# The first block's triangular systems in two halves, and eight chunks' key products moved into the loop

## The chip, the cores and the metric

The kernel runs on one core of one Trainium2 chip. The core has five engines with a queue of instructions each, which run side by side and wait for one another by semaphores: TensorE (PE; its weight loads are listed as PEld), VectorE (DVE), ScalarE (ACT), GpSimd (POOL) and SyncE (SP, which here only issues DMAs). Each queue is worked off in order. The metric is the device time of one execution in microseconds, lower is better; the kernel before has a median of 855.91 us over 3 runs (853.34 to 859.94).

## What is computed

Three stages in a row: a delta-rule attention, a mixing stage with a Fourier transform and an MLP, and a second MLP with a spatial gate. The change touches the first alone:

```python
batch, n_heads, seq, head_dim = 4, 8, 768, 48
k_n = k / (norm(k) + 1e-06)
for t in range(S):
    y[:, :, t] = q[t] @ state
    v_old = state @ k_n[t]
    state = state + beta[t] * outer(k_n[t], v[t] - v_old)
```

## The kernel before

The sequence is cut into 12 chunks of 64 tokens for each of 4 batches, 48 chunks in all, numbered in the order of work. Within a chunk the recurrence becomes a triangular system: with the key products A (key times key, scaled and masked), the kernel needs the inverse of a 64 x 64 unit triangular matrix for each head. It gets the two 32 x 32 diagonal blocks on VectorE and puts the 64 x 64 inverse together on TensorE.

Eight chunks make a block, six blocks in all. VectorE inverts the 32 x 32 systems of one block at a time. `prep` gathers them (tile `Cc`) and transposes them so that each partition holds whole systems (tile `Ts`, 32 rows by 32 columns to a partition). `solve` scales them by beta over the squared norm (line 274), then eliminates in 30 steps. Steps with at least 4 rows and columns on a side are a product into `tm` (line 308) and an addition (line 313), each cut into two pieces; the others go column by column (line 286) or row by row (line 292). A last scaling (line 317) and two transposes (line 327) give `Tc`, back with the heads' rows on the partitions. `norms` slips seven small instructions for the key norms between the steps. `root` is the square root that a block needs before its scaling (line 141, ScalarE).

The head of the program runs once. It loads the keys of chunks 0 to 7, multiplies them (line 187), and solves block 0 on VectorE with nothing else in that queue. Beside it TensorE and ScalarE make the query products of chunks 0 to 7 (line 508) and `stage_a` of chunks 8 to 23: key and query products (line 220), and three ScalarE copies for each chunk (lines 195, 196, 226). One 512-column matmul on zeros follows (`busy`, line 492). Then come `mask_q(0)` (line 241) and `prep(1)`.

The loop has iterations t = -3 to 47. In iteration t: `values(t+2)` scales the values by the norms (ScalarE, line 397); `mask_q`; `stage_d(t)` makes the output and the new state (lines 439, 440; copies 448 and 457); `stage_c(t+1)` (line 420) and its VectorE subtraction `cw` (line 421); `stage_a(t+20)` from chunk 24 on (line 222, copies 195 and 196, one VectorE multiplication in line 229); `diag` and `merge` build the 64 x 64 inverses (TensorE 373 and 375 in bank Z; ScalarE 361, 377, 380); `stage_b(t+2)` (line 405, copy 407). The solve of the next block is dealt out over eight iterations by shares, in three places of an iteration (`part`): block 1 over t = -3 to 4. `chain` makes the order of the code the order of each engine's queue, so nothing overtakes anything within an engine.

Two conditions matter below. Block 1's scaling waits for its square root, which stands in ScalarE's queue at the end of iteration -3, behind that iteration's merges. And `solve` starts the gathering of the next block only when the key products of its chunks have been issued:

```python
while seen_a[0] < 8 * blk + 16:
    yield None
yield from prep(blk + 1)
```

For block 1 that is chunk 23. Before the change `seen_a` stands at 24 when the loop starts.

Of the kernel before, what the change touches and what calls it, by code (L numbers as in the profile page):

```python
# [20 lines left out]
C = 64  # L21
# [9 lines left out]
HEAD = 24  # L31
# [35 lines left out]
class Kernel:  # L67
# [36 lines left out]
    def load(self, out, in_):  # L104
        return self.nc.sync.dma_start(out=out, in_=in_)
# [13 lines left out]
    def attention(self, cp, pg, pe, p, x, filler, after_solves):  # L119
# [1 line left out]
        bt = cp.tile([128, NBC * HP], F32, name="bt")  # L121


        mk = cp.tile([128, 4 * C + 34], F32, name="mk")
# [142 lines left out]
        def solve(blk):  # L267
# [62 lines left out]
                    root(blk + 1)  # L330
            Tts[blk] = Tc

        class Spread:


# [12 lines left out]
                    pass  # L348


        qs = [slice(32 * u, 32 * u + 32) for u in range(4)]
        lo, up = qs[::2], qs[1::2]


# [128 lines left out]
        zz = self.bank("pz", [128, 512])  # L483
        nc.vector.memset(zz, 0.0)
        for t in ZS:
            nc.scalar.copy(out=t[:, :, :32], in_=mk[:, 4 * C + 2 :].unsqueeze(1).to_broadcast([128, 8, 32]))
# [593 lines left out]
    def run(self):  # L1080
# [19 lines left out]
        def after_solves():  # L1100
            ce.__exit__(None, None, None)
            e["cdw"], e["dw"] = self.pool("dw", "right")
            self.sc, self.dc = slot(2, [128, 1281]), slot(9, [97, 386])
            e["cu"], e["u"] = self.pool("mlpu", "right")

            def loads():

                self.load(out=self.sc, in_=a["sc"])
                yield
                self.load(out=self.dc, in_=a["dc"])  # L1110
                self.load(out=self.idn, in_=a["idn"])
# [132 lines left out]
def layout(q, k, v, beta, moe_w_ch1, moe_w_ch2, moe2_w_in, moe2_w_spatial, moe2_b_spatial, moe2_w_out):  # L1244
    f = np.float32
    o = {}
# [35 lines left out]
    o["mk"] = np.concatenate([j + i < C, s2, j < i, s2, s >= 32, s < 32, s % 32 == i[:, :32]], 1).astype(f)  # L1282
    o["idn"] = np.eye(128, dtype=f)


# [67 lines left out]
```

## Time and profile before

| | |
|---|---|
| median of 3 runs | 855.91 us (853.34 to 859.94) |
| the profiled execution, its own time | 856.51 us |
| its span, first to last instruction | 854.7 us |
| TensorE busy | 805.6 us (94%) |
| VectorE busy | 617.3 us (72%) |
| ScalarE busy | 417.9 us (49%) |
| GpSimd busy | 5.5 us (1%) |
| mean granted TensorE clock | 0.978 of full speed |

The shares are means over stages with different limits. VectorE is busy almost throughout the first quarter of the span, TensorE almost throughout the second half. The rows below are taken from the first 76 us, with one view of the whole.

### The profile page before, as it was taken

Reading aid. Unit: us, or ns where it says so; the run is one execution under the profiler, and the core shown is the slowest. Engines: PE = TensorE matmul, PEld = TensorE weight load, DVE = VectorE, ACT = ScalarE, POOL = GpSimd, SP = SyncE. Lnnn points to the kernel's source line nnn. Section 1 sums busy time; section 2 is a strip of 40 time slices with the busy share of each in tenths; the row PEclk is TensorE's granted clock in tenths of the full one; section 3 lists DMA queues with packets and bytes.
Section 4 is the critical chain, followed back from the end, with each engine's and each line's share of the span. In section 5 each row is a group of like instructions: output and inputs, shape, how many; then the busy total and the mean of one; then the engine's idle time right before and its main releaser. Section 6 shows DMA issues by size and latency. Waiting matters only on the chain.

```text
span 854.7 us, 24141 instructions
## 1 busy us (share of the span) xinstructions
PE 805.6 (94%) x9965; PEld 768.5 (90%) x9965; DVE 617.3 (72%) x1852; ACT 417.9 (49%) x1062; POOL 5.5 (1%) x38
## 2 busy tenths in 40 slices
PE   7778999888887999999999999999999999999998
PEld 7667888777787999899999999999999899899998
DVE  6999999997968997783654891526688377486563
ACT  2668888876665644232224451223472362543532
POOL 0000000000000000000000000000000000000000
PEclk9869999998999999999999999999999999999999
DMA  9365666556440600001022411121101101102001
GB/s 225 92 173 162 179 173 186 150 154 170 137 144 22 240 2 1 0 1 29 1 72 78 130 31 27 32 62 56 37 1 47 67 9 46 58 18 67 29 0 56
DMA packets 57951, 67.57 MB, mean 79 GB/s; under 512 B 31857, under 2 KB 48978, under 8 KB 57842
## 3 DMA queue, kind: packets, MB, share of 16 engines
q1 hardware_dynamic: 57698, 65.89, 26.8%
q8 instruction: 78, 1.28, 0.6%
q14 instruction: 31, 0.25, 0.1%
q10 hardware_dynamic: 144, 0.15, 0.1%
HBM read 53.62 MB, written 4.72 MB: 68 GB/s over the span
## 4 chain that ended last, share of the span: by engine, by line
PE 67%; DVE 4%; ACT 1%; issue 1%; ACTq 0%
PE bankX L833 17%; PE bankY L846 15%; PE bankX L1031 10%; PE bankX L1011 6%; PE bankX L979 6%; PE bankY L1059 5%; PE bankV L846 2%; PE bankX L646 2%; PE bankZ L1059 1%; PE bankX L662 1%; PE bankY L420 0%; PE bankY L440 0%; PE bankX L818 0%; PE bankY L405 0%; PE bankX L640 0%
## 5 line engine op out<-in xcount | busy, mean ns | idle before, releaser
L846 PE MATMUL bankY<-w,hx 128*128 128x384 f32 x756 | 147.2, 336 | 0.0
L833 PE MATMUL bankX<-uh,w 128*128 128x384 f32 x504 | 137.7, 340 | 0.7 <-DVE ul L755 0.7
L846 PEld LDWEIGHTS bankY<-w,hx 128*128 128x128 f32 x756 | 132.4, 188 | 0.5 <-issue 0.3
L838 DVE SCALAR_TENSOR_TENSOR hx<-bankX,hx 128x384 fp32r<-128x384 f32 x84 | 46.2, 551 | 76.4 <-ACT hx L837 73.7
L837 ACT ACTIVATE hx<-bankX 128x384 fp32r<-128x384 f32 x84 | 41.2, 491 | 115.0 <-PE bankX L833 110.2
L833 PEld LDWEIGHTS bankX<-uh,w 128*128 128x128 f32 x504 | 92.1, 188 | 1.2 <-DVE ul L755 0.9
L1031 PE MATMUL bankX<-w,A 128*128 128x384 f32 x504 | 88.8, 334 | 0.0
L1031 PEld LDWEIGHTS bankX<-w,A 128*128 128x128 f32 x504 | 87.6, 188 | 0.0
L833 PE MATMUL bankX<-ul,w 128*128 128x384 f32 x252 | 85.1, 338 | 0.0
L313 DVE TENSOR_TENSOR Ts<-Ts,tm 128x110 f32<-128x110 f32 (+26 forms) x264 | 59.0, 260 | 0.9
L308 DVE TENSOR_TENSOR tm<-Ts 128x110 f32<-128x110 f32 (+26 forms) x264 | 58.6, 258 | 0.4
L420 PE MATMUL bankY<-gak,WU 64*64 64x112 f32 x704 | 47.2, 276 | 6.3 <-ACT WU L407 3.2
L405 PE MATMUL bankY<-gak,TT 64*64 64x96 f32 x768 | 45.8, 260 | 7.6 <-ACT gak L397 3.1
L440 PE MATMUL bankY<-WU,gak 64*64 64x48 f32 x768 | 51.6, 230 | 1.3 <-ACT x L457 1.1
L1011 PE MATMUL bankX<-xh,s 128*128 128x384 f32 x192 | 50.0, 338 | 0.0
L405 PEld LDWEIGHTS bankY<-gak,TT 64*64 64x64 f32 x768 | 38.0, 143 | 12.2 <-ACT gak L397 3.6
L439 PE MATMUL bankY<-Sb,cw 48*48 48x48 f32 x640 | 38.4, 210 | 11.1 <-DVE cw L421 10.7
L440 PE MATMUL bankY<-Sb,cw 48*64 48x48 f32 x704 | 47.3, 226 | 1.6 <-DVE cw L421 1.4
L1020 ACT CAST u<-hx 128x384 fp32r<-128x384 f32 x32 | 15.8, 514 | 66.1 <-DVE hx L1018 66.1
L833 PEld LDWEIGHTS bankX<-ul,w 128*128 128x128 f32 x252 | 47.3, 188 | 0.0
L439 PE MATMUL bankY<-WU,gak 64*64 64x48 f32 x704 | 45.8, 227 | 0.3 <-issue 0.3
L979 PE MATMUL bankX<-s,xh 128*128 128x512 f32 x144 | 45.9, 395 | 0.0
(219 smaller groups left out, 1806.1 us busy)
## 6 DMA issues: line engine op xcount, KB each, us to landing
kq<-in_kq_dram SPq DMA_DIRECT2D x24, 448.0 KB, 4.2
qt<-in_qt_dram SPq DMA_DIRECT2D x48, 196.0 KB, 4.0
gak<-in_kv_dram SPq DMA_DIRECT2D x48, 192.0 KB, 4.2
w<-in_w_dram SPq DMA_DIRECT2D x24, 384.0 KB, 6.4
out_dram<-x SPq DMA_DIRECT2D x24, 192.0 KB, 1.9
kq<-in_kc_dram SPq DMA_DIRECT2D x8, 448.0 KB, 10.1
x<-x SPq DMA_DIRECT2D x96, 36.0 KB, 1.9
s<-in_wi_dram SPq DMA_DIRECT2D x6, 512.0 KB, 4.1
```

The source lines that it names most:

```text
L308: nc.vector.tensor_tensor(out=tm, in0=T[:, r, k : k + 1].to_broadcast(sh), in1=T[:, k : k + 1, :k].to_broadcast(sh), op=MUL)
L313: nc.vector.tensor_add(o, o, tm)
L405: nc.tensor.matmul(pb[h, hp].rearrange("p t d -> p (t d)"), lhsT=tt[h, o + hp], rhs=kv[h, hp], start=True, stop=True)
L420: nc.tensor.matmul(pc[h, hp], lhsT=w[h, hp, :C], rhs=gas[bc][h, hp, : C + D], start=True, stop=True)
L439: nc.tensor.matmul(ps[C * i : C * i + n - C, hp], lhsT=k[:, C:n], rhs=u, start=not last, stop=end)
L440: nc.tensor.matmul(po[hs[1 - i], hp], lhsT=k[:, :C], rhs=u, start=not last, stop=end)
L833: nc.tensor.matmul(ph, lhsT=w1[f][i][:, c * 128 : c * 128 + 128], rhs=cur[k][:, c], start=(c + j == 0), stop=(c == 2 and j == 2))
L846: nc.tensor.matmul(acc[t], lhsT=hx[i][:, t * 128 : t * 128 + 128], rhs=w2[e][k], start=(e == 0 and j == 0), stop=(e == 11 and j == 2),)
L979: nc.tensor.matmul(pv, lhsT=xT[t][i][:, c, kk * 128 : kk * 128 + 128], rhs=wi[2 * c + 1][k], start=(c + j == 0), stop=(c == 2 and j == 2))
L1011: nc.tensor.matmul(pu, lhsT=wi[2 * c][i][:, f * 128 : f * 128 + 128], rhs=xT[hf][k][:, c], start=(c + j == 0), stop=(c == 2 and j == 2))
L1031: nc.tensor.matmul(acc, lhsT=A[:, m, o, i, kk], rhs=Bo[name, kk][:, k], start=(kk + j == 0), stop=(kk == 2 and j == 2))
L1059: nc.tensor.matmul(po, lhsT=a[:, :128], rhs=wo[f][k], start=(f + j == 0), stop=(f == last and j == 2))
```

## The change

Block 0 alone is solved by a new function `halves`. VectorE inverts the two 16 x 16 diagonal blocks of each 32 x 32 system side by side (14 steps in place of 30, on at most 56 elements a piece); the 16 x 16 square below them is made by TensorE as a product of three matrices. `right` multiplies the key products by the upper inverse and ScalarE scales and masks the result into `Yh`; `left` puts the old columns back through a unit matrix, adds the product of the lower inverse (`V`, a third transpose) with `Yh`, and ScalarE copies the sum into `Tc`. Both work on a quarter of the heads (`q`): quarters 0 and 1 in the head, the others in iterations -3 to -1. `stage_a` of chunks 16 to 23 goes from the head into iterations -3 to 4, one each, ahead of `stage_a(24)` in iteration 4. The loads of chunks 24 to 28 are issued in iterations -3, -2, 0, 2 and 4 instead of -3 to 1. The unit matrix `idn` is loaded early, one column is added to `mk`.

```diff
+        def halves(blk):
+            Tf, T, sq, n0 = preps.pop(blk)
+            dT, r = scale(blk, sq, n0)
...
+            for b in range(2):
+                nc.vector.scalar_tensor_tensor(
+                    out=T2[:, b], in0=T2[:, b], scalar=-1.0, in1=d2[:, b].unsqueeze(1).to_broadcast(sh2), op0=MUL, op1=MUL
+                )
...
+            for k in range(1, 15):
+                ops = []
+                for b in range(2):
+                    t = T2[:, b]
...
+            V = p.tile([128, 32, 32], F32, name="V", bufs=1)
+            nc.gpsimd.memset(V[:, :, :16], 0.0)
+            nc.vector.transpose(out=V[:, :, 16:].rearrange("p g r -> p r g"), in_=T[:, 16:])
...
+            def right(q):
+                py, ys[q] = self.bank("pd", [128, 8, 16]), p.tile([128, 8, 16], F32, name="Yh", bufs=2)
+                for g in range(8):
+                    h = 8 * q + g
+                    for u, us in enumerate(qs):
+                        c = C + 32 * (u % 2)
+                        nc.tensor.matmul(py[us, g], lhsT=gas[blk * 8 + h // 4][us, h % 4, c : c + 32], rhs=Tc[us, h, :16], start=True, stop=True)
+                nc.scalar.activation(ys[q], py, AF.Copy, scale=mk[:, 4 * C + 34 : 4 * C + 35])
+
+            def left(q):
+                pr, y, o = self.bank("pd", [128, 8, 16]), ys.pop(q), Tc[:, 8 * q : 8 * q + 8, :16]
+                for us in qs:
+                    nc.tensor.matmul(pr[us], lhsT=self.idn[us, us], rhs=o[us], start=True, stop=False)
+                for g in range(8):
+                    for us in qs:
+                        nc.tensor.matmul(pr[us, g], lhsT=V[us, 8 * q + g], rhs=y[us, g], start=False, stop=g == 7)
+                nc.scalar.copy(out=o, in_=pr)
...
-        Spread(solve(0), 0).finish()
+        right, left = halves(0)
...
-        for bc in range(8, HEAD):
+        for bc in range(8, 16):
             stage_a(bc)
         busy(CF["last"], 512)
+        for part, q in ((right, 0), (right, 1), (left, 0), (left, 1)):
+            part(q)
...
+        lead = {-3: HEAD, -2: HEAD + 1, 0: HEAD + 2, 2: HEAD + 3, 4: HEAD + 4}
+        rest = {-3: ((right, 2), (right, 3)), -2: ((left, 2),), -1: ((left, 3),)}
...
             part(c2)
+            if t + R <= HEAD:
+                stage_a(t + R - 1)
+                if t in lead:
+                    load_kq(lead[t])
             if HEAD <= t + R < NBC:
                 stage_a(t + R)
-            if t < T0 + CF["kq"]:
-                load_kq(HEAD + t - T0)
+            for half, q in rest.get(t, ()):
+                half(q)
```

The order of instructions moves in three places. The first is VectorE's queue in the head: of before, the start of block 0's elimination (the first of 24 steps with `tm` stands in the last four rows).

```order
L274 SCALAR_TENSOR_TENSOR Ts<-Ts,dT 128x16x16
L274 SCALAR_TENSOR_TENSOR Ts<-Ts,dT 128x512
L286 SCALAR_TENSOR_TENSOR Ts<-Ts 128x30
L286 SCALAR_TENSOR_TENSOR Ts<-Ts 128x29 x2
L286 SCALAR_TENSOR_TENSOR Ts<-Ts 128x28 x3
L162 TENSOR_TENSOR nw<-n_221 128x32
L308 TENSOR_TENSOR tm_242<-Ts 128x52
L308 TENSOR_TENSOR tm_244<-Ts 128x56
L313 TENSOR_TENSOR Ts<-Ts,tm_242 128x13x4
L313 TENSOR_TENSOR Ts<-Ts,tm_244 128x14x4
```

Of the change, the end of the same stretch: the last of its 10 steps with `tm`, the row steps, the scaling, the transposes, and what follows.

```order
L366 TENSOR_TENSOR tm_304<-Ts 128x36
L366 TENSOR_TENSOR tm_306<-Ts 128x36
L372 TENSOR_TENSOR Ts<-Ts,tm_304 128x3x12
L372 TENSOR_TENSOR Ts<-Ts,tm_306 128x3x12
L360 SCALAR_TENSOR_TENSOR Ts<-Ts 128x13 x4
L360 SCALAR_TENSOR_TENSOR Ts<-Ts 128x14 x2
L376 TENSOR_TENSOR Ts<-Ts,dT 128x16x16 x2
L379 STREAM_TRANSPOSE Tc<-Ts 128x16x32 x2
L382 STREAM_TRANSPOSE V<-Ts 128x16x32
L241 TENSOR_TENSOR gak<-gak,mk 128x8x64
```

The queue has 60 rows fewer, all of them here; a third transpose stands ahead of `mask_q(0)`. The second place is ScalarE's queue between the head and block 1's square root (line 141). Of before:

```order
L226 COPY gak<-bankX 128x4x64
L377 ACTIVATE ZS_84<-bankZ 96x8x32
L361 COPY TT_89<-Tc 32x8x32 x2
L377 ACTIVATE ZS_85<-bankZ 96x8x32
L380 COPY TT_89<-bankZ 32x512 x2
L141 ACTIVATE n_747<-sq 128x32
```

Of the change, with the lines of the merges 74 higher (377 is 451, 361 is 435, 380 is 454):

```order
L394 ACTIVATE Yh<-bankY,mk 128x128 x2
L404 COPY Tc<-bankY 128x8x16 x2
L451 ACTIVATE ZS_84<-bankZ 96x8x32
L435 COPY TT_89<-Tc 32x8x32 x2
L195 ACTIVATE gak<-bankX,mk 128x4x32
L196 COPY gak<-bankX 128x4x32
L226 COPY gak<-bankX 128x4x64
L394 ACTIVATE Yh<-bankY,mk 128x128 x2
L451 ACTIVATE ZS_85<-bankZ 96x8x32
L454 COPY TT_89<-bankZ 32x512 x2
L141 ACTIVATE n_799<-sq 128x32
```

Nine more instructions stand between block 0's inverse and the square root. The third place is VectorE's queue in iterations 3 and 4, where block 2 is gathered (line 254). Of before, from the last scaling of block 1 the queue goes on with a gathering, `cw`, a gathering, as the trace's rows below show in time. Of the change, line 495 being `cw`:

```order
L317 TENSOR_TENSOR Ts<-Ts,dT 128x512 [waits DVE_49]
L495 TENSOR_TENSOR cw<-qt,bankY 112x448 [waits DMAHW0_49,PE_49]
L241 TENSOR_TENSOR gak<-gak,mk 128x8x64
L229 TENSOR_TENSOR gak<-bankX,mk 128x4x64 [waits DMAHW1_49,DMAHW5_49,PE_49,Activation_49]
L254 SCALAR_TENSOR_TENSOR Cc<-gak,mk 128x512 x2
L261 STREAM_TRANSPOSE Ts<-Cc 128x1024 [waits DVE_49]
L263 COPY sq<-Ts 128x32 [waits DVE_49]
L327 STREAM_TRANSPOSE Tc<-Ts 128x16x32 x2
```

Both gatherings now stand behind `mask_q(6)` and the multiplication of `stage_a(24)`, because `seen_a` reaches 24 only with `stage_a(23)` in iteration 4.

## Rows read from the trace of the kernel before

**Rows 1.** Windows by stretch: start:end, length, each engine's busy us (instructions), granted clock, DMA.

```profile
15.00:76.00 61.00, 46.77 (x1096) 42.70 (x1098) 58.97 (x265) 40.26 (x131) 1.65 (x12) 0.80 0.54 140
76.00:200.00 124.00, 113.04 (x3366) 100.47 (x3360) 114.25 (x470) 100.60 (x311) 2.63 (x19) 0.97 0.61 169
300.00:855.00 555.00, 548.74 (x3150) 535.50 (x3148) 351.54 (x875) 211.19 (x454) 0.00 (x0) 1.00 0.12 37
```

**Rows 2.** Timeline, VectorE, block 0: start us, us, line, operation, tiles, shapes, count [idle].

```profile
14.72 1.02 DVE L274 SCALAR_TENSOR_TENSOR Ts<-Ts,dT 128x256 f32<-128x256 f32 x2
15.78 1.31 DVE L286 SCALAR_TENSOR_TENSOR Ts<-Ts 128x30 f32<-128x30 f32 x6
17.12 0.34 DVE L308 TENSOR_TENSOR tm<-Ts 128x52 f32<-128x52 f32 x2
17.38 0.33 DVE L313 TENSOR_TENSOR Ts<-Ts,tm 128x52 f32<-128x52 f32 x2
...
36.10 1.97 DVE L327 STREAM_TRANSPOSE Tc<-Ts 128x512 f32<-128x512 f32 x2
37.96 0.65 DVE L241 TENSOR_TENSOR gak<-gak,mk 128x512 f32<-128x512 f32 x1
```

**Rows 3.** Timeline, VectorE, start of block 1, first cw, end of block 1.

```profile
43.52 0.18 DVE L153 TENSOR_SCALAR w<-n 128x32 f32<-128x32 f32 x1 [1.40 <-ACT n L141]
...
57.15 0.61 DVE L421 TENSOR_TENSOR cw<-qt,bankY 112x448 f32<-112x448 f32 x1
...
69.89 0.74 DVE L254 SCALAR_TENSOR_TENSOR Cc<-gak,mk 128x512 f32<-128x512 f32 x1
...
72.78 0.68 DVE L241 TENSOR_TENSOR gak<-gak,mk 128x512 f32<-128x512 f32 x1
73.39 2.10 DVE L327 STREAM_TRANSPOSE Tc<-Ts 128x512 f32<-128x512 f32 x2
...
75.68 0.18 DVE L153 TENSOR_SCALAR w<-n 128x32 f32<-128x32 f32 x1
```

**Rows 4.** Timeline, ScalarE: chunks 15 and 16, then iterations 1 to 4.

```profile
26.03 0.37 ACT L195 ACTIVATE gak<-bankX,mk 128x128 f32<-128x128 f32 x1
...
26.90 0.37 ACT L195 ACTIVATE gak<-bankX,mk 128x128 f32<-128x128 f32 x1
...
59.67 0.32 ACT L448 COPY Sb<-bankY 128x192 f32<-128x192 f32 x1 [3.90 <-PE bankY L440]
...
64.29 1.01 ACT L397 ACTIVATE gak<-gak,n_all 128x48 f32<-128x48 f32 x4
...
67.67 1.01 ACT L397 ACTIVATE gak<-gak,n_all 128x48 f32<-128x48 f32 x4
...
71.60 1.01 ACT L397 ACTIVATE gak<-gak,n_all 128x48 f32<-128x48 f32 x4
...
73.52 0.23 ACT L141 ACTIVATE n<-sq 128x32 f32<-128x32 f32 x1
73.65 0.35 ACT L195 ACTIVATE gak<-bankX,mk 128x128 f32<-128x128 f32 x1
```

**Rows 5.** Windows, merge instructions alone (bank Z); engines PE, PEld, DVE, ACT.

```profile
39.65:41.65 2.00, 1.93 (x64) 1.69 (x64) 0.00 (x0) 0.00 (x0) 0.50 0.62 152
61.50:62.65 1.15, 1.10 (x64) 0.93 (x64) 0.00 (x0) 0.00 (x0) 1.00 0.00 0
```

**Rows 6.** Windows around falls of the granted clock, columns as in Rows 1.

```profile
34.10:37.00 2.90, 0.00 (x0) 0.00 (x0) 2.83 (x9) 0.00 (x0) 0.00 (x0) 1.00 0.00 0
44.00:54.00 10.00, 8.96 (x168) 8.11 (x166) 9.78 (x56) 7.21 (x22) 0.15 (x1) 0.50 0.97 237
54.00:57.70 3.70, 0.00 (x0) 0.00 (x0) 3.70 (x17) 1.73 (x6) 0.00 (x0) 0.96 0.17 44
57.80:60.50 2.70, 2.68 (x72) 2.68 (x74) 2.70 (x15) 0.79 (x3) 0.00 (x0) 0.50 0.65 209
```

**Rows 7.** Timeline, TensorE, the matmul on zeros behind the last head chunk.

```profile
32.90 1.13 PE L492 MATMUL bankY<-TT 128*128 128x512 f32 x2
```

More of the change, by code (lines that the diff above doesn't have):

```diff
@@ L121, in attention @@
         bt = cp.tile([128, NBC * HP], F32, name="bt")
-        mk = cp.tile([128, 4 * C + 34], F32, name="mk")
+        mk = cp.tile([128, 4 * C + 35], F32, name="mk")
         ZS = [cp.tile([128, 8, 64], F32, name=f"ZS{i}") for i in range(2)]
@@ L331, in solve @@
             Tts[blk] = Tc
+        qs = [slice(32 * u, 32 * u + 32) for u in range(4)]
+        def halves(blk):
+            Tf, T, sq, n0 = preps.pop(blk)
+            dT, r = scale(blk, sq, n0)
+            T2 = Tf.rearrange("p (b x) -> p b x", b=2)[:, :, :512].rearrange("p b (i c) -> p b i c", c=32)[:, :, :, :16]
+            d2 = dT.rearrange("p (b i) -> p b i", b=2)
+            sh2 = [128, 16, 16]
+            for b in range(2):
+                nc.vector.scalar_tensor_tensor(
+                    out=T2[:, b], in0=T2[:, b], scalar=-1.0, in1=d2[:, b].unsqueeze(1).to_broadcast(sh2), op0=MUL, op1=MUL
+                )
+            nc.gpsimd.memset(Tf[:, 0:1024:33], 1.0)
+            nc.gpsimd.memset(T[:, 16:, :16], 0.0)
+            newton = norms(blk, sq, n0, r)
+            for k in range(1, 15):
+                ops = []
+                for b in range(2):
+                    t = T2[:, b]
+                    if k < 3:
+                        for c in range(k):
+                            nc.vector.scalar_tensor_tensor(
+                                out=t[:, k + 1 :, c], in0=t[:, k + 1 :, k], scalar=t[:, k, c : c + 1], in1=t[:, k + 1 :, c], op0=MUL, op1=ADD
+                            )
+                    elif k > 12:
+                        for i in range(k + 1, 16):
+                            nc.vector.scalar_tensor_tensor(
+                                out=t[:, i, :k], in0=t[:, k, :k], scalar=t[:, i, k : k + 1], in1=t[:, i, :k], op0=MUL, op1=ADD
+                            )
+                    else:
+                        o, sh = t[:, k + 1 :, :k], [128, 15 - k, k]
+                        tm = pe.tile([128, 256], F32, name=f"tm{b}", bufs=2)[:, : sh[1] * k].rearrange("p (i j) -> p i j", j=k)
+                        nc.vector.tensor_tensor(
+                            out=tm, in0=t[:, k + 1 :, k : k + 1].to_broadcast(sh), in1=t[:, k : k + 1, :k].to_broadcast(sh), op=MUL
+                        )
+                        ops.append((o, tm))
+                next(newton, None)
+                for o, tm in ops:
+                    nc.vector.tensor_add(o, o, tm)
+            for _ in newton:
+                pass
+            for b in range(2):
+                nc.vector.tensor_mul(T2[:, b], T2[:, b], d2[:, b].unsqueeze(2).to_broadcast(sh2))
+            Tc = pg.tile([128, 32, 32], F32, name="Tc", bufs=2)
+            for s in (slice(0, 16), slice(16, 32)):
+                nc.vector.transpose(out=Tc[:, :, s].rearrange("p g j -> p j g"), in_=T.rearrange("p i j -> p j i")[:, s])
+            V = p.tile([128, 32, 32], F32, name="V", bufs=1)
+            nc.gpsimd.memset(V[:, :, :16], 0.0)
+            nc.vector.transpose(out=V[:, :, 16:].rearrange("p g r -> p r g"), in_=T[:, 16:])
+            Tts[blk] = Tc
+            ys = {}
+            def right(q):
[14 more added lines that the diff above has]
+                nc.scalar.copy(out=o, in_=pr)
+            return right, left
@@ L348, in finish @@
                     pass
-        qs = [slice(32 * u, 32 * u + 32) for u in range(4)]
         lo, up = qs[::2], qs[1::2]
@@ L472, in attention @@
             load_kq(8 + 2 * i)
+        load(out=self.idn, in_=a["idn"])
         load(out=qx, in_=a["qx"].rearrange("b p h -> p b h"))
@@ L485, in attention @@
         for t in ZS:
-            nc.scalar.copy(out=t[:, :, :32], in_=mk[:, 4 * C + 2 :].unsqueeze(1).to_broadcast([128, 8, 32]))
+            nc.scalar.copy(out=t[:, :, :32], in_=mk[:, 4 * C + 2 : 4 * C + 34].unsqueeze(1).to_broadcast([128, 8, 32]))
         warm = TT[0].rearrange("p a b -> p (a b)")
@@ L1110, in loads @@
                 self.load(out=self.dc, in_=a["dc"])
-                self.load(out=self.idn, in_=a["idn"])
                 for i in range(CF["ahead"]):
@@ L1281, in layout @@
     j, s2 = KEY[s], np.where(s < 32, (s <= i) & (i < 32), (i < 32) | (s <= i))
-    o["mk"] = np.concatenate([j + i < C, s2, j < i, s2, s >= 32, s < 32, s % 32 == i[:, :32]], 1).astype(f)
+    o["mk"] = np.concatenate([j + i < C, s2, j < i, s2, s >= 32, s < 32, s % 32 == i[:, :32], -(s % 32 >= 16).astype(f)], 1).astype(f)
     o["idn"] = np.eye(128, dtype=f)
```

## The prediction

> **What bounds the kernel now.** I read the windows by stretch first. From 15 to 76 us VectorE is busy 58.97 of 61.00 us, TensorE 46.77 and ScalarE 40.26 [rows 1]; from 76 to 200 us VectorE and TensorE are both near 92%; behind 300 us TensorE alone binds, 548.74 of 555 us. So the change works where VectorE is the bound. The order of every queue is fixed, and behind iteration 4 it is the same as before: what block 2 gains or loses at its start is carried to the end. Transfers don't hold it up there (DMA share 0.12 behind 300 us). The time that counts is therefore the first VectorE instruction of block 2's scaling, at 75.68 us [rows 3], and the question is how much earlier it comes.
>
> Then VectorE's timeline. Block 0's elimination runs from 14.72 to `mask_q(0)` at 37.96 us, 23.24 us without a gap that the reader could fill [rows 2]. The chunks' copies beside it take ScalarE 0.87 us a chunk (26.03 to 26.90) [rows 4], so they hide. Behind it VectorE waits once, 1.40 us, for block 1's square root on ScalarE, and starts block 1 at 43.52 us [rows 3]. That instruction is what the head has to release.
>
> **What VectorE saves in the head.** Two scalings of 512 elements in all, for 768 in 1.06 us: 0.7 us each [rows 2]. Six column instructions, as many as before, 1.24 us; six row instructions the same at most. Forty product and addition instructions of 36 to 56 elements; the rows show two of 52 and 56 elements in 0.26 us, 0.13 each, so 5.2 us, and seven norm instructions among them at most 0.9. Two transposes 1.86 us, the third half of that, 0.93. The sum is 12.8 us at these prices. The operands are smaller than in the rows, which takes off something; if all per-element time were halved it would be about 11.5. I take 12.3, nearer to the rows. `mask_q(0)` then starts at 27.0 instead of 37.96: **11.0 us saved** (10.4 to 11.7). `Tc` is ready at 26.1. The gathering of block 1 behind it needs chunk 15, copied by 26.9, so it doesn't wait.
>
> **What the path to block 1 gains.** TensorE comes off `stage_a(15)` when ScalarE begins to read it, about 26 us. The 512-column matmul of 1.13 us [rows 7], hidden so far behind the elimination, now stands on the path: `right(0)` starts at 27.0, not 26.1. A `right` is 32 matmuls, which the trace lists as 64. Sixty-four merge matmuls on 32 partitions took 1.93 us at 1.2 GHz and 1.10 at 2.4 GHz [rows 5]; they have 32 and 64 columns, these have 16. I take half, 0.55 us, between 0.3 (only columns count) and 1.1 (only the count does). A `left` has four matmuls of 128 columns more: 0.8 (0.5 to 1.4). Two of each are 2.7 us, the last result and its copy 0.6: ready at 30.3.
>
> The Trainium skill ("TensorEngine Tiling (Array Packing)", "Instruction Overhead") has about 60 cycles of overhead on every matmul and says that a shorter free dimension saves nothing below that. By it 16 columns cost as much as 32, the four parts take about 1.1 us more, and the gain worked out below would be 0.5 us. No row of before has 16 columns, so the trace does not decide it.
>
> From `Tc` (36.10 + 1.97 = 38.07) to 43.52 the chain through two merges, `diag` and the square root took 5.45 us, at half clock. At full clock the 64-matmul merge saves 0.83 us [rows 5] and the shorter one about half of it: 4.2. New in that chain on ScalarE are `stage_a(16)`, 0.87, and two `Yh` copies like the first of a chunk's, 0.37 each at most, 0.65 together. So 30.3 + 4.2 + 0.9 + 0.6 gives 36.0: **block 1 starts 7.5 us earlier**, not 11.0. TensorE has no long pause on this way (it was busy from 15 us on), so I take full clock. At half clock the four parts cost 4.8, the merges 5.45, and about 0.7 of `right(2)` and `right(3)` shows: 40.0, only 3.5 us earlier.
>
> **What the loop gives back.** Seven and a half microseconds earlier, `cw(1)` is at 49.65 instead of 57.15 [rows 3]. Until there ScalarE is no limit: it was busy 8.94 of 13.7 us from 44 to 57.7 [rows 6] and gets three chunks (2.6) and two quarter copies (0.6), 12.1 us. TensorE still pauses before `cw(1)`, as at 54.0 to 57.7, where the clock fell afterwards to 1.2 GHz [rows 6]; I take the same fall. ScalarE's copy of the state then starts at 59.67 - 7.5 = 52.2 us.
>
> From there ScalarE decides, and this is the step that costs most. Block 2's gathering was interleaved with iterations 3 and 4; now it stands behind `stage_a(23)` in iteration 4. Before, ScalarE went from 59.67 through 64.29, 67.67 and 71.60 to 73.52, where iteration 4's chunk comes: 4.62 + 3.38 + 3.93 + 1.92 = 13.85 us [rows 4]. Into it go chunks 20, 21 and 22, 3 x 0.87 = 2.6, and the first two copies of chunk 23, about 0.4. So the second gathering can start 16.85 us behind the state copy, at 69.1 us, against 69.89 before. Meanwhile VectorE is done with block 1's steps 7.5 us early and idles for most of that. From the second gathering to the end of block 1's transposes it was 73.39 + 2.10 - 69.89 = 5.6 us, less 0.6 for `mask_q(6)`, which now stands ahead [rows 3]: 5.0. That ends at 74.1. The multiplication of `stage_a(24)` has gone ahead too, so block 2's scaling starts at once, 74.1 instead of 75.68: **1.6 us earlier**.
>
> **Edits at nothing.** GpSimd's new memsets run beside VectorE's steps. The early load of `idn` stands before `qx`, the sign column and the query tiles in SP's queue; its first user is `left(0)` near 28 us, that of the others later. The loads of chunks 24 to 28 wait in SP's queue for TensorE to have read chunks 15, 17, 19, 21 and 23; behind them stand value and query loads. Chunk 24 is wanted near 69 us and its load goes out near 31, so it is covered; if a value load came late instead, `values` would wait and ScalarE's chain would lengthen by as much. The merge behind block 1's transposes still comes after them, so it moves with them.
>
> **The sum.** 856.51 - 1.6 = 854.9 us against the profiled execution; this one is 0.6 above the median of the three runs, so 854.3 on their scale. The runs lie 6.6 us apart, more than the effect.
>
> **Rivals.** *The wait on ScalarE is mostly slack (0.22).* Part of the 13.85 us were waits for TensorE, 3.90 us stood before the state copy, and at full clock near `cw(1)` the copy comes about 1 us earlier and iteration 1 is 1 us shorter. With these two the gain is 3.6. If `cw(1)` held ScalarE up no more than its own work does, it would reach the state copy 12.1 us and one `values`, 1.0, behind block 1's start, at 49.1 us, and the second gathering 16.85 later at 66.0: a gain of 4.7, 851.8 (851.2 on the scale of the median). For it: TensorE has less to do in the head. Against: every copy waits for a matmul of its own iteration.
>
> *Slower (0.20).* TensorE falls to 1.2 GHz in the head and stays there. Then block 1 starts at 40.0, all that follows is 4.0 us later than in my sum, and the time is 858.9 (858.3 on the scale of the median). It decides from the point where block 1's first scaling stands later than 37.6 us, 36.0 + 1.6. For it: from 44 to 54 us TensorE was busy 8.96 of 10 us with just such small matmuls, and the clock stayed at 0.50 the whole time [rows 6]. Against: that stretch began with a pause from 34.1 to 37.0 us [rows 6], which is gone. The Trainium skill ("TensorE: Matmul & The Clock Gate", "What's actually happening") says that activity releases the throttle. By it the small matmuls would hold full clock, my sum; the row from 44 to 54 us does not agree with it.
>
> *The saving goes through whole (0.04).* 11.0 us, 845.5. It would need square root and gathering to follow VectorE without delay, and the order of the queues forbids both.
>
> **How the numbers follow.** My forecast, a gain between 0 and 3.5 us, has 0.52: 852.5 to 856 on the median's scale. The slack has 0.22 (849.5 to 852.5), the slower case 0.20 (856 to 860), the whole saving 0.04, a delay beyond all this 0.02. The range leaves out the ends: 850.0 to 859.0. A change of over 1%, 8.6 us, is about what a measurement of this kernel can tell from none; only the whole saving and a tail of the slack reach it on one side (0.05), a half clock that lasts through the loop on the other (0.04).
>
> **What would show it.** `mask_q(0)` near 27.0 us and the first `right` matmul at 27.0, about 1 us behind `Tc`. Block 1's scaling near 36.0 us behind a wait of 4 to 5 us for the square root. In iterations 3 and 4 a new wait of VectorE for ScalarE or TensorE, several us long, ahead of the multiplication of `stage_a(24)` or the second gathering. Block 2's scaling near 74 us, and from there the same spacing as before. I am wrong if block 2's gathering doesn't wait, if block 1's scaling stands before 34 or behind 38 us, or if the shift at 74 us is not the shift at the end.

## The result: slower, by TensorE's instructions and a held gathering

| | before | after |
|---|---|---|
| median of the runs compared | 857.25 us (853.34 to 859.94) | 866.63 us (866.29 to 867.01) |
| ratio to before | 1 | 1.0113 (1.0070 to 1.0156) |
| span of the profiled execution | 854.7 us | 864.5 us |
| TensorE, VectorE, ScalarE busy | 805.6, 617.3, 417.9 us | 811.7, 606.2, 419.8 us |

Forecast were 854.3 us and a range up to 859.0. VectorE lost the 11 us of work that it was to lose, and the kernel still became 9 us slower. In the profile after, lines of the loop are 74 higher than before, 153, 241 and 254 are the same. VectorE's timeline (start, duration, engine, line, operation, out<-in, shape, count; in brackets the idle time before and what ended it) tells where:

```profile
14.35 0.76 DVE L343 SCALAR_TENSOR_TENSOR Ts<-Ts,dT 128x256 f32<-128x256 f32 x2
...
25.86 0.66 DVE L241 TENSOR_TENSOR gak<-gak,mk 128x512 f32<-128x512 f32 x1
...
43.98 0.18 DVE L153 TENSOR_SCALAR w<-n 128x32 f32<-128x32 f32 x1 [13.96 <-ACT n L141]
...
69.95 0.68 DVE L241 TENSOR_TENSOR gak<-gak,mk 128x512 f32<-128x512 f32 x1
76.29 0.42 DVE L229 TENSOR_TENSOR gak<-bankX,mk 128x256 f32<-128x256 f32 x1 [5.66 <-ACT gak L196]
76.63 1.40 DVE L254 SCALAR_TENSOR_TENSOR Cc<-gak,mk 128x512 f32<-128x512 f32 x2
...
82.07 0.15 DVE L153 TENSOR_SCALAR w<-n 128x32 f32<-128x32 f32 x1
```

`mask_q(0)` stands at 25.86 us in place of 37.96 [rows 2]: 12.1 us saved. All of it is gone at block 1's scaling, 43.98 against 43.52 [rows 3], behind a wait of 13.96 us for the square root. Then block 2's gathering is held for 5.66 us, and block 2's scaling stands at 82.07 against 75.68 [rows 3], 6.4 us late. The next block's scaling comes at 124.2 against 115.1, 9.1 late, and the end 9.8 late.

Why the square root was late is in TensorE's timeline of the same execution ("issue" is idle time in which the engine waited for nothing that the profile shows):

```profile
26.41 0.79 PE L393 MATMUL bankY<-Tc,gak 32*32 32x16 f32 x72
27.67 0.62 PE L393 MATMUL bankY<-Tc,gak 32*32 32x16 f32 x54 [0.47 <-issue]
...
28.34 0.72 PE L403 MATMUL bankY<-Yh,V 32*32 32x16 f32 x64
30.96 0.42 PE L400 MATMUL bankY<-Tc,idn 32*32 32x128 f32 x8 [1.89 <-issue]
...
34.96 1.64 PE L393 MATMUL bankY<-Tc,gak 32*32 32x16 f32 x108 [0.71 <-issue]
...
40.34 0.26 PE L447 MATMUL bankZ<-Tc,gak 32*32 32x32 f32 x1 [3.44 <-issue]
```

Four stops, 6.5 us together, and none of them ends with an operand that arrives. The last stands within the merges ahead of the square root, and ScalarE's timeline shows what it holds up:

```profile
42.14 0.38 ACT L451 ACTIVATE ZS<-bankZ 96x256 f32<-96x256 f32 x1 [4.94 <-PE bankZ L449]
...
43.72 0.23 ACT L141 ACTIVATE n<-sq 128x32 f32<-128x32 f32 x1
```

Windows from one stop to the next show how much ran between them (busy us and, in brackets, instructions; matmuls and weight loads apart):

```profile
30.90:34.80 3.90, 3.29 (x128) 2.81 (x128) 0.00 (x0) 2.18 (x7) 0.00 (x0) 0.73 0.22 55
34.90:40.20 5.30, 1.94 (x128) 1.70 (x128) 0.00 (x0) 0.73 (x2) 0.00 (x0) 0.50 0.48 126
```

Twice 128 and 128, 256 instructions. And the DMA view of the window from 28.70 to 30.97 us, around the second stop, has one packet in it, of the queue that brings instructions (queue, kind: packets, MB, share):

```profile
q8 instruction: 1, 0.02, 2.6%
```

In the window from 37.00 to 40.35 there is one such packet again, beside 54 of loads. So the reading is: TensorE ran out of instructions. They come in pieces of 256, and TensorE worked off the three pieces between the stops in 1.4, 3.3 and 1.9 us (27.67 to 29.06, 30.96 to 34.25, 34.96 to 36.90). The times of the packets in the trace bear it out: the last one ahead of the end of each stop is in at 26.27, 29.74, 33.58 and 39.02 us, and TensorE goes on 1.2 to 1.4 us behind it. The same holds for all 53 of TensorE's stops of 0.3 us or more that end in "issue" within the first 130 us of the fourteen kernels of this document: each ends 1.2 to 1.7 us behind such a packet. What sets the start of a packet is not shown; that of the longest stop began 1.0 us into it, with loads moving beside it.

Before has a stop of this kind too, with one such packet in it. It ended at 15.33 us, and the rows that the prediction was read from begin at 14.72:

```profile
15.33 0.86 PE L187 MATMUL bankX<-gak 48*64 48x64 f32 x22 [3.15 <-issue]
```

The Trainium skill ("Runtime: NRT & Kernel Launch", "Instruction fetch mechanics") names pieces of 16 KiB, 256 instructions, and calls the crossing mostly hidden. The piece agrees with the trace; here the crossing was not hidden, it cost 0.47 to 3.44 us each time.

The granted clock (third from the right in each row of the windows) fell with it:

```profile
26.00:30.00 4.00, 2.60 (x202) 2.00 (x200) 3.93 (x5) 1.25 (x4) 0.00 (x0) 1.00 0.21 64
30.00:34.00 4.00, 3.04 (x124) 2.67 (x128) 0.02 (x1) 1.45 (x4) 0.67 (x5) 0.84 0.07 17
34.00:38.00 4.00, 2.19 (x138) 1.85 (x136) 0.00 (x0) 1.53 (x5) 0.00 (x0) 0.50 0.79 205
38.00:42.00 4.00, 1.66 (x58) 1.50 (x58) 0.00 (x0) 0.00 (x0) 0.00 (x0) 0.50 0.02 6
```

2.4 GHz until the second stop, and 1.2 GHz from about 33 us on. The profile alone can't say which of the stops, the clock, the held gathering and ScalarE's longer queue cost the time.

### The profile page after: what moved, and what is told of

It reads as the page before. It is cut to its first block, busy times and chain, and to the rows that moved or that the text cites. A ratio compares the mean times of both kernels' runs of the same rounds, so it can differ in the third digit from the quotient of the medians.

```text
span 864.5 us, 25181 instructions
## 1 busy us (share of the span) xinstructions
PE 811.7 (94%) x10509; PEld 772.6 (89%) x10509; DVE 606.2 (70%) x1797; ACT 419.8 (49%) x1070; POOL 6.3 (1%) x40
## 4 chain that ended last, share of the span: by engine, by line
PE 79%; DVE 9%; ACT 7%; issue 4%; DMA 1%; SPq 0%; ACTq 0%; DVEq 0%
PE bankX L917 17%; PE bankY L930 15%; PE bankX L1115 10%; PE bankX L1095 6%; PE bankX L1063 6%; PE bankY L1143 5%; PE bankY L494 3%; PE bankY L479 2%; PE bankZ L449 2%; PE bankX L222 2%; PE bankV L930 2%; PE bankX L730 2%; PE bankY L514 1%; PE bankY L513 1%; PE bankX L220 1%
## 5 line engine op out<-in xcount | busy, mean ns | idle before, releaser
L514 PE MATMUL bankY<-WU,gak 64*64 64x48 f32 x768 | 49.5, 222 | 1.4 <-ACT x L531 1.4
L313 DVE TENSOR_TENSOR Ts<-Ts,tm 128x108 f32<-128x108 f32 (+10 forms) x216 | 48.8, 261 | 0.9
L308 DVE TENSOR_TENSOR tm<-Ts 128x108 f32<-128x108 f32 (+10 forms) x216 | 48.5, 260 | 0.4
L494 PEld LDWEIGHTS bankY<-gak,WU 64*64 64x64 f32 x704 | 35.9, 137 | 13.1 <-issue 7.4
L514 PE MATMUL bankY<-Sb,cw 48*64 48x48 f32 x704 | 44.9, 220 | 1.4 <-DVE cw L495 1.4
L1063 PE MATMUL bankX<-s,xh 128*128 128x512 f32 x144 | 45.9, 395 | 0.0
L513 PE MATMUL bankY<-WU,gak 64*64 64x48 f32 x704 | 43.5, 220 | 0.9 <-issue 0.8
```

Source lines behind the costliest of these rows:

```text
L308: nc.vector.tensor_tensor(out=tm, in0=T[:, r, k : k + 1].to_broadcast(sh), in1=T[:, k : k + 1, :k].to_broadcast(sh), op=MUL)
L313: nc.vector.tensor_add(o, o, tm)
L494: nc.tensor.matmul(pc[h, hp], lhsT=w[h, hp, :C], rhs=gas[bc][h, hp, : C + D], start=True, stop=True)
L513: nc.tensor.matmul(ps[C * i : C * i + n - C, hp], lhsT=k[:, C:n], rhs=u, start=not last, stop=end)
L514: nc.tensor.matmul(po[hs[1 - i], hp], lhsT=k[:, :C], rhs=u, start=not last, stop=end)
L1063: nc.tensor.matmul(pv, lhsT=xT[t][i][:, c, kk * 128 : kk * 128 + 128], rhs=wi[2 * c + 1][k], start=(c + j == 0), stop=(c == 2 and j == 2))
```

## Experiments

Landmarks of all kernels, in us from the start of each span (first instruction of a block's scaling on VectorE):

| kernel | block 1 | block 2 | block 3 | span |
|---|---|---|---|---|
| before | 43.5 | 75.7 | 115.1 | 854.7 |
| after | 44.0 | 82.1 | 124.2 | 864.5 |
| e1_move | 44.9 | 85.4 | 127.8 | 872.4 |
| e2_halves | 50.7 | 83.0 | 122.6 | 860.7 |
| e3_gate | 43.7 | 78.3 | 117.8 | 857.9 |
| e4_root | 33.3 | 81.8 | 124.1 | 868.7 |
| e5_code | 45.9 | 78.5 | 117.9 | 857.0 |
| e6_norest | 40.0 | 80.2 | 122.8 | 862.9 |
| e7_cand | 34.9 | 79.9 | 119.3 | 859.4 |
| e8_thin | 33.0 | 73.8 | 120.4 | 857.7 |
| e9_cover | 43.9 | 82.4 | 123.7 | 864.6 |
| e10_gatethin | 33.3 | 66.8 | 109.9 | 845.8 |
| e11_wide | 42.5 | 74.8 | 114.2 | 855.6 |
| e12_bf16 | 37.9 | 72.1 | 111.8 | 853.8 |

### The two parts of the change, each alone

e1_move takes from the change only the eight chunks that go into the loop, with the loads; block 0 is solved as before.

```diff
-        for bc in range(8, HEAD):
+        for bc in range(8, 16):
             stage_a(bc)
...
+            if t + R <= HEAD:
+                stage_a(t + R - 1)
...
```

> Only the second part of the change: block 0 solved as before, stage_a of chunks 16 to 23 in iterations -3 to 4. Theory (the gathering of block 2 behind chunk 23 costs most of it, through ScalarE): block 1's scaling stays near 43.5 us; from the first state copy (near 59.7 us) to the second gathering it is some 17 us as in the changed kernel, so VectorE waits 4 to 6 us ahead of the multiplication of stage_a(24) and block 2's scaling stands near 81 to 82 us (75.7 before, 82.1 in the change); 6 to 10 us slower than before at the end, ratio 1.007 to 1.012. Rival (the loss comes from the halves and TensorE's stalls in the head): block 2's scaling within 1.5 us of 75.7, ratio 0.998 to 1.002.

Measured 1.0174 (1.0135 to 1.0212), more than expected. Block 2's gathering is held for 5.67 us here too:

```profile
79.56 0.42 DVE L229 TENSOR_TENSOR gak<-bankX,mk 128x256 f32<-128x256 f32 x1 [5.67 <-ACT gak L196]
```

e2_halves takes only the new solution of block 0; all of `stage_a` stays in the head.

```diff
-        for bc in range(8, 16):
+        for bc in range(8, HEAD):
             stage_a(bc)
...
```

> Only the first part: block 0 in halves, all 16 stage_a in the head ahead of right and left. Theory (TensorE stops for instructions between the small matmuls of right, left and the merges): right starts near 33 us, and 16 to 18 us pass from there to block 1's scaling as in the change (27 to 44), so it stands at 48 to 51 us, 5 to 7 later than before; VectorE isn't held in iteration 4; block 2's scaling at 79 to 83 us, 4 to 7 us slower at the end, ratio 1.004 to 1.008. Rival (only the place of the key products matters): block 1's scaling at 41 to 44 us and the time within 2 us of before or below it, ratio 0.996 to 1.002.

Measured 1.0116 (1.0073 to 1.0159), above the 1.004 to 1.008 that was expected, though block 1 and block 2 stand where they were expected:

```profile
50.70 0.18 DVE L153 TENSOR_SCALAR w<-n 128x32 f32<-128x32 f32 x1 [20.12 <-ACT n L141]
```

Block 1's scaling is 7.2 us later than before, behind a wait of 20.12 us, and TensorE's stops are there (2.32, 1.07 and 2.38 us between 37 and 48 us), without any chunk moved. So each part costs by itself, and the two are not additive (1.7 and 1.2% alone, 1.1% together).

### The held gathering

e3_gate is the change with chunks 16 to 23 multiplied by iteration 1, so that `seen_a` is at 24 before block 2's gathering is due.

```diff
+        early = {-3: (16,), -2: (17,), -1: (18, 19), 0: (20, 21), 1: (22, 23)}
...
-            if t + R <= HEAD:
-                stage_a(t + R - 1)
+            for bc in early.get(t, ()):
+                stage_a(bc)
...
```

> The change, but the key products of chunks 16 to 23 are made in iterations -3, -2 (one each), -1, 0 and 1 (two each), so that block 2 may be gathered in iterations 3 and 4 as before. Theory (held gathering): block 1's scaling stays near 44 us, the 5.7 us wait of VectorE in iteration 4 goes, block 2's scaling at 77 to 79 us against 82.1, the end 4 to 7 us faster than the change, ratio to before 1.002 to 1.006. Rival (ScalarE's sum of work decides wherever it stands): the waits move to iterations 0 to 2, block 2's scaling at 81 us or later, ratio 1.009 to 1.012.

Measured 1.0047 (1.0024 to 1.0069). Neither gathering waits now, and the gatherings stand in iterations 3 and 4 again:

```profile
72.50 0.74 DVE L254 SCALAR_TENSOR_TENSOR Cc<-gak,mk 128x512 f32<-128x512 f32 x1
...
78.27 0.23 DVE L153 TENSOR_SCALAR w<-n 128x32 f32<-128x32 f32 x1
```

Block 1's scaling stays where it was, block 2's comes 3.8 us earlier, the span is 6.6 us shorter. The hold is a real cost, and about 0.5% is left.

### Is it the square root, or TensorE?

e4_root puts block 1's square root directly behind its gathering, ahead of the merges in ScalarE's queue.

```diff
         for _ in prep(1):
             pass
+        root(1)
...
-                root(1)
```

> The change, with block 1's square root right behind prep(1) in the head instead of at the end of iteration -3. Theory (ScalarE's chain, which starts when the first merged inverse is there, sets block 2): block 1's scaling moves from 44.0 to about 32.3 us, but block 2's scaling stays within 1.5 us of 82.1 and the time within 2 us of the change's, ratio to before 1.009 to 1.013. Rival (the late start of block 1 on VectorE is the loss): block 2's scaling 6 to 11 us earlier, ratio 0.998 to 1.004.

Measured 1.0171 (1.0137 to 1.0205), above the 1.009 to 1.013 that was expected and in any case no faster than the change. Block 1 starts 10.6 us earlier, and VectorE then stands at iteration 0's `cw` (L495) and again at the gathering:

```profile
33.34 0.18 DVE L153 TENSOR_SCALAR w<-n 128x32 f32<-128x32 f32 x1 [3.11 <-ACT n L141]
...
54.47 0.62 DVE L495 TENSOR_TENSOR cw<-qt,bankY 112x448 f32<-112x448 f32 x1 [7.39 <-PE bankY L494]
...
76.06 0.42 DVE L229 TENSOR_TENSOR gak<-bankX,mk 128x256 f32<-128x256 f32 x1 [5.66 <-ACT gak L196]
```

So block 2 is not set by when VectorE starts block 1. The first of these waits is for TensorE, whose second merge goes on at 41.3 us here, as late as in the change; the second is the held gathering. That the late merges set both is argued. Block 3 stands where it does in the change (124.1 us), so what is lost beyond it comes later and stays unexplained; TensorE's mean clock from 130 to 300 us was 0.95 here and in e1_move, 0.99 in the change. e7_cand (e2_halves with the early square root, right and left behind it) says the same.

> A version that may beat both: block 0 in halves, all 16 stage_a in the head as before, and block 1's square root ahead of right and left, so that VectorE starts block 1 when chunk 23 is copied. Theory: block 1's scaling near 34 us, 9.5 earlier than before; right, left and merges are late by TensorE's instruction supply, so the first state copy and ScalarE's chain gain only some; block 2's scaling between 72 and 76 us, the end 0 to 4 us faster than before, ratio 0.995 to 1.000. Rival (TensorE's late merges decide everything): block 2's scaling at 78 us or later, ratio 1.003 to 1.007.

It measured 1.0052 (1.0027 to 1.0077), as the rival had it: 34.9 us for block 1, then 10.54 us of waiting for TensorE at that `cw`.

```profile
59.14 0.62 DVE L495 TENSOR_TENSOR cw<-qt,bankY 112x448 f32<-112x448 f32 x1 [10.54 <-PE bankY L494]
```

### Do instructions run out?

e5_code puts 128 matmuls of 32 x 32 x 16 on zeros into before, where TensorE waits for `Tc` from 34 us on; e11_wide puts two of 512 columns there.

```diff
         busy(CF["last"], 512)
+        py = self.bank("pd", [128, 8, 16])
+        for i in range(32):
+            for us in qs:
+                nc.tensor.matmul(py[us, i % 8], lhsT=warm[us, :32], rhs=warm[us, :16], start=True, stop=True)
         mask_q(0)
```

```diff
         busy(CF["last"], 512)
+        busy(2, 512)
         mask_q(0)
```

> The kernel before, with 128 added 32 x 32 matmuls of 16 columns on zeros behind the 512-column matmul of the head, where TensorE has nothing to do from 34 to 38 us; nothing reads them and they wait for nothing but their bank. They take about 2.2 us at the pace of right in the changed kernel (64 of the trace's matmuls in 0.6 to 0.7 us without a stop), so they fit into the pause. Theory (TensorE gets its instructions in pieces of 16 KB, and small matmuls use a piece up faster than the next one comes): stops of 1 to 3.5 us that nothing in the program explains, among the added matmuls or in the merges behind them, each ending behind a transfer of the instruction queue; block 1's scaling 1 to 4 us later than 43.5. Rival (the stops in the change belong to the data of right and left: their copies, banks or transposes): no new stop over 0.3 us, block 1's scaling at 42.5 to 43.6 us.

> Before, with two more 512-column matmuls on zeros where the earlier run put 128 small ones: as much TensorE time, hardly any instructions. Theory, the stops come by count of instructions: no stop of over 1 us between 33 and 45 us (2.25 us there with the 128 small ones). Rival, any added work of TensorE there brings a stop or a delay of the same size: 1.5 to 2.5 us.

TensorE's timeline of the first:

```profile
35.16 1.83 PE L516 MATMUL bankY<-TT 32*32 32x16 f32 x196
39.23 0.88 PE L516 MATMUL bankY<-TT 32*32 32x16 f32 x51 [2.25 <-issue]
```

and of the second:

```profile
33.48 2.84 PE L492 MATMUL bankY<-TT 128*128 128x512 f32 x6
38.22 0.69 PE L373 MATMUL bankZ<-Tc,gak 32*32 32x32 f32 x32 [1.90 <-DVE Tc L327]
```

The small ones, which wait for nothing and take part in nothing, stop for 2.25 us; the wide ones don't stop, and the 1.90 us behind them are a wait for `Tc`. Block 1's scaling is at 45.9 with the former, 42.5 with the latter. e5_code's end moved little, 1.0019 (0.9995 to 1.0042); e11_wide was run once and has no interval.

e6_norest leaves quarters 2 and 3 of right and left out, and with them half of block 0's lower squares.

> The change without right and left of quarters 2 and 3 (the square stays zero for chunks 4 to 7, a part of the inverse is left out): 272 fewer of TensorE's matmuls as the program counts two to one in the trace, work of about 2 us by itself. Theory (instruction supply): the stop of 3.4 us at the second merge goes or shrinks to under 1 us, block 1's scaling at 38 to 40.5 us against 44.0, and ScalarE's chain and block 2's scaling follow by 3 to 5 us: 77 to 79 us; ratio to before 1.003 to 1.008. Rival (stops have another cause): block 1's scaling at 41.5 us or later, only the 2 us of the work itself gained.

The stop of 3.44 us is gone and block 1's scaling comes at 40.0, as expected, but the gathering is still held (5.66 us). Block 2 at 80.2 us and the ratio, 1.0104 (1.0058 to 1.0150), are worse than the 77 to 79 us and 1.003 to 1.008 that were expected: the ratio hardly moves.

e8_thin is the change with the columns of right and left in an eighth of the matmuls: one of 128 columns for a 32-row group, not eight of 16. One head's matrix serves all eight heads, so it leaves the real lower squares of block 0 out.

```diff
-                for g in range(8):
-                    h = 8 * q + g
-                    for u, us in enumerate(qs):
-                        nc.tensor.matmul(py[us, g], lhsT=gas[blk * 8 + h // 4][us, h % 4, c : c + 32], rhs=Tc[us, h, :16], start=True, stop=True)
+                h = 8 * q
+                for u, us in enumerate(qs):
+                    nc.tensor.matmul(py[us], lhsT=gas[blk * 8 + h // 4][us, h % 4, c : c + 32], rhs=Tc[us, h : h + 8, :16], start=True, stop=True)
...
```

> The change, but right and left issue one 128-column matmul for each 32-row group in place of eight of 16 columns (one head's matrix for all eight heads, so the lower squares of block 0 are not the real ones): 40 matmuls in all instead of 272, the copies stay. Theory A, TensorE's many small matmuls, the stops for their instructions and the clock fall set the head: the stops between 26 and 45 us sum to under 3 us (6.5 in the change), block 1's scaling stands at 33 to 37 us, block 2's at 74 to 77, ratio to before 0.998 to 1.003. Rival B, ScalarE's copies of chunks 16 to 23 in the loop are enough for the delay: block 1's scaling is as early, but VectorE still waits 4 to 6 us in iteration 4, block 2's scaling stays at 80 to 82, ratio 1.006 to 1.011.

Its windows, and VectorE's timeline:

```profile
26.00:30.00 4.00, 3.90 (x126) 2.98 (x130) 3.86 (x5) 2.48 (x9) 0.01 (x1) 1.00 0.14 44
30.00:34.00 4.00, 3.40 (x115) 2.76 (x97) 0.86 (x4) 3.93 (x14) 0.67 (x5) 1.00 0.79 213
34.00:38.00 4.00, 3.13 (x86) 2.48 (x84) 3.82 (x22) 3.91 (x16) 0.16 (x1) 1.00 1.01 246
38.00:42.00 4.00, 4.00 (x131) 3.57 (x120) 4.00 (x27) 3.52 (x11) 0.00 (x0) 1.00 0.59 145
```

```profile
33.04 0.18 DVE L153 TENSOR_SCALAR w<-n 128x32 f32<-128x32 f32 x1 [3.10 <-ACT n L141]
...
67.95 0.42 DVE L229 TENSOR_TENSOR gak<-bankX,mk 128x256 f32<-128x256 f32 x1 [5.69 <-ACT gak L196]
...
73.75 0.14 DVE L153 TENSOR_SCALAR w<-n 128x32 f32<-128x32 f32 x1
```

No stop of over 0.3 us that ends in "issue" between 26 and 46 us, full clock throughout, block 1 at 33.0 and block 2 at 73.75: 8.3 us earlier than in the change. Theory A held for the head; the hold stays, as its rival said. Stops and clock went together in this run, so their shares are not told apart; the four parts themselves took 1.8 us (26.27 to 28.08) in place of 3.2. The ratio is 1.0034 (1.0000 to 1.0067), just above what theory A gave (0.998 to 1.003), because block 3 follows block 2 at 46.7 us in place of 39.4. In that stretch TensorE stops once more for 2.23 us, up to 94.7 us, and its clock is at 0.50 in two places.

e10_gatethin joins e3_gate with e8_thin.

> The run with chunks 16 to 23 multiplied by iteration 1, and with the few wide matmuls in right and left in place of the small ones (again not the real lower squares). Theory A: neither the hold nor the many instructions: no wait over 1 us in iteration 4, block 2's scaling at 72 to 75.5 us, ratio 0.994 to 1.000. Rival B, ScalarE's copies alone delay block 2: scaling at 77 to 79 us as in the run with the early chunks, ratio 1.003 to 1.006.

Measured 0.9925 (0.9897 to 0.9953), 847.54 us, and block 2's scaling is earlier than either theory had it:

```profile
66.75 0.17 DVE L153 TENSOR_SCALAR w<-n 128x32 f32<-128x32 f32 x1
```

With e3_gate (859.5) and e8_thin (859.4) this makes a square of medians: 866.6 with both costs, 859.5 without the hold, 859.4 without the many matmuls, 847.5 without either. By these each is worth about 7 us while the other is there and 12 when it is gone. The kernels were run in three sessions, so the ratios to each session's own runs of before are the safer measure: 6 to 7 us and 9 to 10. That each cost is larger without the other, by 0.4%, is not clear of the intervals.

Of the 8.9 us that block 2 gains on before, 5.2 are left at block 3, which follows at 43.1 us. In that stretch TensorE stops for 1.95 us at the same place in its instructions as in e8_thin, ten microseconds earlier; first e8_thin, then e10_gatethin:

```profile
94.72 0.24 PE L518 MATMUL bankY<-Sb,qx 48*1 48x48 f32 x1 [2.23 <-issue]
...
84.77 0.20 PE L518 MATMUL bankY<-Sb,qx 48*1 48x48 f32 x1 [1.95 <-issue]
```

### What comes behind the hold

Behind block 2's scaling, block 3's follows at 42.1 us in place of 39.4. e9_cover fills TensorE's idle time from 76 to 82 us, to keep its clock up.

```diff
                 stage_d(t)
+                if t == 5:
+                    busy(5, 512)
```

> The change, with five 512-column matmuls on zeros (1.1 us each) put into TensorE's queue in iteration 5 ahead of block 2's first merge, where TensorE waits from 76 to 82 us. Theory: behind the held gathering another 2.5 to 2.9 us are lost because TensorE starts again at half clock; with the cover the granted clock of 80 to 88 us is above 0.9, block 2's scaling stays at 82, the state copy that stood at 91.7 comes at 89 to 90, and the ratio to before falls to 1.007 to 1.010. Rival: the further loss is the order of VectorE's and ScalarE's instructions there, not the clock: the copy stays at 91 to 92 and the ratio at 1.011.

It did not settle the matter. The added matmuls ended at 80.9 us, TensorE waited 1.72 us, and the clock still fell a little later (windows at 2 us):

```profile
82.00:84.00 2.00, 1.43 (x46) 1.39 (x48) 1.78 (x7) 1.20 (x4) 0.00 (x0) 0.92 0.03 8
84.00:86.00 2.00, 2.00 (x13) 1.72 (x10) 1.78 (x5) 0.52 (x2) 0.16 (x1) 0.50 0.40 104
```

Block 3 follows at 41.3 us, 0.8 better, and the ratio is 1.0133 (1.0102 to 1.0164), no better than the change. e3_gate, which has no hold, has no such loss (39.5 us), nor have e2_halves (39.6) and e7_cand (39.4). So the 2.7 us go with the hold, while the longer spacing of e10_gatethin, without a hold, goes with its stop; that the 2.7 us come of the clock is argued, not shown.

### A version that beats both

e12_bf16 is e3_gate with the whole computation and half the instructions in right and left: bf16 operands (which round them), no unit matrix, and VectorE adds the product to `Tc`.

```diff
-                        nc.tensor.matmul(py[us, g], lhsT=gas[blk * 8 + h // 4][us, h % 4, c : c + 32], rhs=Tc[us, h, :16], start=True, stop=True)
+                        nc.tensor.matmul(py[us, g], lhsT=gb[us, h, c : c + 32], rhs=Tb[us, h], start=True, stop=True)
...
-                nc.scalar.copy(out=o, in_=pr)
+                nc.vector.tensor_add(o, o, pr)
```

> A candidate with the whole computation: the run with chunks 16 to 23 multiplied by iteration 1, and right and left with half the TensorE instructions: their operands are copied to bf16 (keys by ScalarE in the head, the upper columns and V by VectorE), the unit matrix is left out and VectorE adds the product to Tc, behind the gathering of block 1. 256 matmuls stay, with 512 instructions in place of 1088. Theory A, the count of instructions is what costs: the stops between 26 and 45 us fall from 5.0 us to under 2.5, block 1's scaling stands at 35 to 40 us, block 2's at 70 to 75, ratio 0.993 to 1.000. Rival B, the number of matmuls costs, whatever they are made of: block 1's scaling stays at 42 to 44, block 2's at 77 to 79, ratio 1.003 to 1.006.

```profile
37.90 0.18 DVE L154 TENSOR_SCALAR w<-n 128x32 f32<-128x32 f32 x1 [6.79 <-ACT n L142]
...
72.14 0.16 DVE L154 TENSOR_SCALAR w<-n 128x32 f32<-128x32 f32 x1
```

Block 1 at 37.9, block 2 at 72.1, one stop of 0.86 us on TensorE in place of e3_gate's 1.92 and 3.08, and that one ends behind block 1's scaling:

```profile
38.90 0.34 PE L405 MATMUL bankY<-Yh,Vb 32*32 32x16 bf16 x25 [0.86 <-issue]
```

This run also helps to tell stops and clock apart. Its clock is down as well, as the first of these windows shows, the second being e3_gate's:

```profile
34.00:38.00 4.00, 4.00 (x106) 3.45 (x95) 0.10 (x1) 2.84 (x10) 0.00 (x0) 0.50 0.98 219
34.00:38.00 4.00, 2.98 (x146) 2.42 (x142) 0.00 (x0) 1.90 (x6) 0.00 (x0) 0.50 0.84 216
```

So against e3_gate block 1 gains 5.8 us (37.9 against 43.7) with the clock at 0.50 in both from 32 or 33 us on. The stops, and with them the halved work in right and left, cost that much without the clock; how the 5.8 us divide between these two is not shown.

Measured 855.45 us, 0.9962 (0.9943 to 0.9981) of before and about 1.5% under the change.

## Why the prediction was wrong

**VectorE's saving** was right and a little small: 12.1 us, not 11.0, just outside the stated 10.4 to 11.7. The new solution took 11.5 us (14.35 to 25.86), forecast 12.3, and it began 0.4 us earlier than the old one (14.35 against 14.72), which the forecast did not have.

**The four parts** were nearly right while TensorE ran. Without the stops they took 3.2 us (26.41 to 29.06 and 30.96 to 31.93, less the stop of 0.47), forecast 2.7. Two `right` took 1.41 us, 0.7 each, not 0.55. The rule of the Trainium skill ("TensorEngine Tiling (Array Packing)", "Instruction Overhead") that was weighed there gave an estimate of about 3.8 for the four; the trace lies between.

**"TensorE has no long pause on this way (it was busy from 15 us on), so I take full clock"** is the step that failed. I counted columns and waits for operands, and took for granted that a busy engine has its instructions. The trace of before had the sign, the stop of 3.15 us up to 15.33. In the change TensorE stopped for 6.5 us, and the clock fell behind the second stop. Block 1's scaling stood at 44.0, not 36.0. With the same columns in few matmuls (e8_thin) it stood at 33.0 at full clock. These 8.0 us, and 3.4 that are lost behind block 2 on balance (below), are the whole miss in span: 864.5 us against 854.7 - 1.6 = 853.1.

**What the loop gives back** was right. From the state copy at 59.97 us to the second of the two gatherings at 77.3 it took 17.3 us, forecast 16.85, and the new wait of VectorE, "several us long, ahead of the multiplication of `stage_a(24)`", is the one of 5.66. From there to block 2's scaling 4.8, forecast 5.0. So block 2 stands at 82.1, 8.0 us behind the forecast 74.1, just as block 1 is 8.0 behind 36.0. In one point the chain was drawn wrong: I let VectorE's start of block 1 release all that follows. e4_root moved that start by 10.6 us and nothing followed; the wait that took its place is for TensorE. In e8_thin, where the merges are on time, block 2 comes at 73.75, close to the forecast. But its two legs there were 3 us shorter and 3 us longer than in the sum, so the agreement is in part luck.

**"From there the same spacing as before"** failed too, by 2.7 us to block 3 and 1.9 more to block 4, of which 1.2 came back later. The page of before could not show it, since nothing is held there.

**The rivals.** *Slower* had the right sign and half of the mechanism: 1.2 GHz in the head. Its price was 4.0 us, block 1 at 40.0; it had no stops in it. The argument against it, that the pause ahead of such a stretch is gone, was overtaken by a pause of another kind. The row it was argued from, 44 to 54 us of before, was read too freely: of its 168 listed matmuls 64 are those of a merge, and the others have 48 to 112 columns. *The wait on ScalarE is mostly slack* can be judged by e3_gate and e10_gatethin: taking the hold away gives 6 to 10 us by the ratios, so the wait is dear, but only once the chunks come earlier. *The whole saving* needs both costs away: e10_gatethin, which leaves the real squares out, gained 8.9 us of span and 0.75% (0.47 to 1.03).

## What to carry to other kernels

Where a change replaces vector work by many small matmuls, count TensorE's instructions beside its columns. If pieces of 256 are used up as fast as here (1.4 to 3.3 us), price the gaps from the rows that end in "issue", or make fewer and wider matmuls. Look for such rows ahead of the stretch that is changed as well: the one of before stood mostly ahead of the rows that were read. When work is moved behind a gate that another engine's queue waits for, open the gate earlier in the same change; the held gathering cost about as much as the instructions did. And a gain on the engine that is busiest counts only up to the next engine's queue: follow the release and not the busy share.

## What the runs showed of the hardware

In before, no stop of TensorE's matmuls between 33 and 45 us ends in "issue"; 128 small matmuls without any operand to wait for brought one of 2.25 us, and two wide ones brought none. A 32 x 32 x 16 matmul in fp32 is listed twice, each with a weight load; in bf16 once (64 for two quarters of `left`, in 0.66 us). The stops move with the count: with fewer instructions in the head, e8_thin had its next one up to 94.7 us, in a stretch where the change had none, and e10_gatethin had it at the same matmul, up to 84.8 us. TensorE went on 1.2 to 1.7 us behind the last packet of instructions in each of the 53 stops of 0.3 us or more that end in "issue".
